# A fused attention and gated feed-forward block on one core: first query tile by key halves, first LayerNorm on VectorE alone, feed-forward weights shared by tiles 0 and 1

## The chip, the core and the metric

The kernel runs on one core of a Trainium2 chip. A core has five engines, each with its own queue of instructions that it works through in order: TensorE (PE: matmul, with weight loads, PEld, that overlap), VectorE (DVE), ScalarE (ACT), GpSimd (POOL) and SyncE (SP), which here issues nearly all DMAs. They meet only at semaphores. Matmul results land in PSUM, from where VectorE or ScalarE copies them to SBUF, the working memory of 128 partitions. The metric is the device time of one execution in microseconds (us), lower is better.

## The reference

The input x has 2048 tokens of width 1024, in bf16. There are 32 query heads of width 32 and a single key/value head that all of them share.

```
def _A_ref(x, wq, wk, wv, wo):
    q = (x @ wq).reshape(B, S, H, Dh) -> (B, H, S, Dh)
    k = x @ wk                       # one head for all
    v = x @ wv
    p = softmax(q k^T * Dh ** -0.5)  # over all 2048 keys, no mask
    return heads_joined(p @ v) @ wo
def _B_ref(x, w_gate, w_up, w_down):
    h = sigmoid(x @ w_gate) * (x @ w_up)     # width 3584
    return h @ w_down
h  = x + _A_ref(layernorm(x), ...)
h2 = h + _B_ref(layernorm(h), ...)
```

## The kernel before

**Order of work.** The program builds its instruction lists with a planner (class Plan, line 37): every operation is given an estimated duration, its dependencies and a priority, a simulated clock decides which operation an engine takes next, and what comes out is a fixed list for each engine, with semaphore waits put in from the dependencies. The loop from line 878 on chooses for TensorE: a score visit if ScalarE has less than 750 ns of work ahead, with a PV block after it if one is ready; otherwise matmuls of the first group that is ready in the order of PRIO (line 376): transposes, K/V, the first Q groups, output projection, gate/up, down, other Q groups. If nothing is ready it plans a filler matmul (line 944; before the first visit that of line 939), which is why fillers show where TensorE had no work.

**Units.** Tokens are cut into 16 tiles of 128. A tile's heads are cut into four pairs of head groups, so there are 64 values of G; G // 4 is the query tile. A visit (G, kq) computes the scores of that pair against 256 keys (emit_S, line 547): 8 small matmuls into PSUM, then two exponentials on ScalarE (line 571), each 128 x 1024, into slots of Pr. Before the change the visits go through G in order and through all eight key blocks kq within it (line 523), and slot u % 16 is used by exponential u. Thus the first pair needs all keys within its eight visits.

**Softmax sums and PV.** VectorE adds the eight key blocks of exponentials into Ts (flush_sums, line 588: seven additions for each of two halves). mk_PV (line 609) makes two blocks of 32 matmuls per G, one for each half of the keys; the second also holds 8 matmuls of a matrix of ones with Ts, which give the row sums. The copies at lines 633 to 645 join the halves, invert the sums and write OT. P slots are reused once their PV block and their addition are done (s_ready, line 531).

**Around attention.** The first LayerNorm is the loop of lines 355 to 367: statistics and centring on VectorE, two pow operations on GpSimd (339, 341), the scale on ScalarE or VectorE as SCALE_ON says. Tiles 0 to 5 (NPT) are transposed on TensorE with a ScalarE copy (line 391), the others by DMA transposes issued from SyncE (line 404). mk_Q (457) computes Q for a head group; all but the first 256 tokens' Q goes through a scratch tensor in DRAM (477) and comes back a tile at a time (516). mk_OP (698) is the output projection and second LayerNorm, flush_hT (725) its transposed copy hnT, mk_GU (788) one item of gate or up, mk_D (840) the down projection.

**Weights.** Each gate or up item for a panel p of 512 columns needs four pieces of 256 KB (USES). A ring of 22 slots keeps pieces; refill (752) replaces the one whose next use is furthest, and ITEMS runs the seven panels upwards for even tiles and downwards for odd ones. The ring shares its memory with x. Weight loads are put into one first-in-first-out line (pace, 244) that pump (248) empties at a planned rate: 260 bytes per ns, and PACE = 205 once more than 64 visits are done. Into the same line go wo (496) and the 28 pieces of w_down (486), the last of these when all Q groups are done (free_wd, 505); gate/up of tile 0 waits for that too (line 835).

Of the kernel before, what the change touches and what calls it, by code (L numbers as in the profile page):

```python
# [9 lines left out]
F32 = mybir.dt.float32  # L10
# [3 lines left out]
P = 128  # L14
# [114 lines left out]
def bass_sequential_preLN__grouped_kv_mqa__glu_gated_glu__prompt_kernel(  # L129
# [22 lines left out]
    ITEMS = [(p, w) for t in range(NT) for p in (range(NFP) if t % 2 == 0 else reversed(range(NFP))) for w in range(2)]  # L152
# [5 lines left out]
    NPS = 16  # L158
    NB = 3
# [4 lines left out]
    USES = [(p, w, d) for p, w in ITEMS for d in range(NPI)]  # L164
# [4 lines left out]
    with ExitStack() as es:  # L169
# [59 lines left out]
        NQS = NFT * 256 // 512  # L229
        half = cst[:, 0:1]  # L230
        negone = cst[:, 1:2]
# [16 lines left out]
        def pump(t):  # L248
            while paced and t >= next_piece[0] and pl.dma_free["sp"] < t + 2500.0:
# [5 lines left out]
                next_piece[0] = max(next_piece[0] + nbytes / (PACE if 64 < v < NV else 260.0), t - 1000.0)  # L255
# [14 lines left out]
        c1 = pl.op("pool", lambda: POOL.memset(negone, -1.0), [c0], occ=60)  # L270
        c2 = pl.op("pool", lambda: POOL.memset(ident[:, :], 0.0), [c1], occ=200)
# [7 lines left out]
        wq_ld = []  # L279

        def load_x(ts):
            sl = slice(ts[0] * P, (ts[-1] + 1) * P)
            o = dma(lambda: SP.dma_start(x_sb[:, ts[0]:ts[-1] + 1, :], xf[sl, :].rearrange("(a p) n -> p a n", p=P)),
                    f"x{ts[0]}", P * D * 2 * len(ts), prio=0)
            for t in ts:
                x_ld[t] = o

        def load_wq(k):
            wq_ld.append(dma(lambda: SP.dma_start(
                wq_sb[:, :, k * 512:(k + 1) * 512],  # L290
                A_wq[:, k * 512:(k + 1) * 512].rearrange("(a p) n -> p a n", p=P)), f"wq{k}", D * 512 * 2, prio=0))
# [6 lines left out]
                    ring="act")  # L298
        load_x([2, 3])
        load_x([4, 5])  # L300
        load_x([6, 7])
        load_wq(0)
        load_x([8, 9])
        load_x([10, 11])
        load_x([12, 13, 14, 15])
        load_wq(1)
# [9 lines left out]
        def stats(ph, ts, srcs, deps, prio):  # L316
            cs = []
            for t, src, dep in zip(ts, srcs, deps):
# [19 lines left out]
            nb = negone if n == 1 else negone.to_broadcast([P, n])  # L338
            g = pl.op("pool", lambda: POOL.tensor_tensor(
                out=dsb[:, ph, sl], in0=zb[:, ph, sl], in1=hb, op=ALU.pow), [f, c0], prio=prio - 1, occ=720, lat=840)  # L340
            h = pl.op("pool", lambda: POOL.tensor_tensor(  # L341
                out=rstd[:, ph, sl], in0=dsb[:, ph, sl], in1=nb, op=ALU.pow), [g, c1], prio=prio - 1, occ=540, lat=660)
            return e, h
# [10 lines left out]
        SCALE_ON = ["dve"] + ["act"] * 7 + ["dve", "act"] * 2 + ["dve"] * 4  # L354
        for ts in [[0], [1]] + [[t, t + 1] for t in range(2, NT, 2)]:
            sv = stats(0, ts, [x_sb[:, t, :] for t in ts], [[x_ld[t]] for t in ts], 3)
            for t in ts:
# [43 lines left out]
        NPT = 6  # L401
# [8 lines left out]
        def queue_after_xT(t):  # L410
# [5 lines left out]
            if t == 3:  # L416
                for g in range(NG):
                    queues["Q"].append(mk_Q(g, 256, 256))
            if t % 4 == 3 and t > 3:
                for g in range(NG):  # L420
                    queues["Q"].append(mk_Q(g, (t // 4) * 512, 512))
# [3 lines left out]
        q_left = [4 * NG + NG]  # L425
        q_left4 = [2 * NG, NG, NG, NG]
# [30 lines left out]
        def mk_Q(g, tok, n):  # L457
# [4 lines left out]
            def after(b, last):  # L462
# [8 lines left out]
                else:  # L471
# [4 lines left out]
                    ev = evac(fa, fd, n, deps, 4)  # L476
# [6 lines left out]
            first = lambda: [wq_ld[g // 4]] + [xT_ev[k] for k in range(tok // P, (tok + n) // P)]  # L483
# [7 lines left out]

        def early_loads(last):
            n = 5 * NG - q_left[0]
            if n in (10, 12):
                k = (n - 10) // 2
                for g in range(4 * k, 4 * k + 4):
                    pace(lambda g=g: SP.dma_start(wo_sb[:, g, :], A_wo[g * P:(g + 1) * P, :]), f"wo{k}", P * D * 2,
                         [last, xT_ev[NT - 1]], wo_ld)
# [24 lines left out]
        visits = [(G, kq) for G in range(NT * ND) for kq in range(VPG)]  # L523
# [3 lines left out]
        slot_add = {}  # L527
        pv_done = {}
        n_exp_of = collections.Counter()

        def s_ready(v):
# [6 lines left out]
            for i in range(2):  # L538
                own = slot_owner.get((2 * v + i) % NPS)
                if own is not None and (own not in pv_done or slot_add.get((2 * v + i) % NPS) is None):  # L540
                    return None
# [3 lines left out]
            return deps  # L545

        def emit_S(v):
# [14 lines left out]
            for i in range(2):  # L562
                u = 2 * v + i
                slot = u % NPS
                own = slot_owner.get(slot)
                free = [pv_done[own], slot_add[slot]] if own is not None else []
# [5 lines left out]
                    out=Pr[:, slot, :].rearrange("p (a b) -> p a b", a=2), in_=S_ps[:, pb:pb + 2, :],  # L572
# [13 lines left out]
        sum_todo = collections.deque((G, kq) for G in range(NT * ND) for kq in range(1, VPG))  # L586

        def flush_sums():
            while sum_todo:
                G, kq = sum_todo[0]  # L590
                if n_exp_of[G] <= kq or (kq == 1 and G > 1 and (G - 2, 1) not in pv_done):
                    return
                sum_todo.popleft()
                for i in range(2):
                    T = Ts[:, G % 2, i * 1024:(i + 1) * 1024]
                    ins = [kq - 1, kq] if kq == 1 else [kq]
                    src = [Pr[:, slot_of[(G, q, i)], :] for q in ins]
                    deps = [exp_of[(G, q, i)] for q in ins]
                    deps.append(pv_done.get((G - 2, 1)) if kq == 1 else sum_ev[(G, kq - 1, i)])
# [5 lines left out]
                    sum_ev[(G, kq, i)] = o  # L605

        oc_ev = {}

        def mk_PV(G, h):
            qb, g = G // ND, 2 * (G % ND)  # L610

            def block(b):
                r = []
                for kt in range(8 * h, 8 * h + 8):
                    kq, kk = kt // KB, kt % KB
                    for j in range(4):
                        slot = slot_of[(G, kq, j // 2)]
                        co = (j % 2) * 512 + kk * 256
                        r.append(mm(F_ps[DH * j:DH * (j + 1), b, 0:256], Vb[:, kt, :], Pr[:, slot, co:co + 256],
# [434 lines left out]
```

## Time and profile before

Three executions took 1127.34 to 1129.27 us, median 1128.49. The profiled one took 1126.47 us, of which the span from first to last instruction is 1124.7 us; the granted TensorE clock averaged 0.998.

| Engine | busy us | share of span | instructions |
|---|---|---|---|
| TensorE matmul | 1069.6 | 95% | 12163 |
| TensorE weight load | 478.9 | 43% | 12347 |
| VectorE | 873.7 | 78% | 1690 |
| ScalarE | 1022.9 | 91% | 1165 |
| GpSimd | 49.1 | 4% | 84 |

| Group (line) | count | busy us | mean ns |
|---|---|---|---|
| exponentials, ScalarE (571) | 1024 | 961.9 | 1056 |
| later row-sum additions, VectorE (601) | 768 | 509.0 | 677 |
| first row-sum additions, VectorE (601) | 128 | 85.4 | 681 |
| gate/up matmuls with ring weights (379) | 1659 | 414.3 | 381 |
| down matmuls (379) | 839 | 208.9 | 380 |
| tanh, ScalarE (817) | 112 | 71.1 | 635 |
| LN1 scale on ScalarE (363) | 9 | 10.0 | 1141 |
| LN1 scale on VectorE (366) | 7 | 3.2 | 480 |
| reciprocal of row sums, VectorE (640) | 64 | 12.3 | 192 |

Busy time counts overlapping instructions once, so a mean can exceed the spacing: a matmul of 381 ns in the table is followed by the next after some 0.22 us. Some matmul records are missing from the trace. A busy TensorE is not one at its peak, and fillers count as busy. In forty equal slices of the span, the busy tenths of ScalarE and the share of the DMA engines are:

```
ACT  6799989999999999999999999999999999999210
DMA  7776188887959597786959596796959596875992
```

ScalarE is full from the fifth slice until near the end; the last exponential starts at 1045.0 us. The first starts at 30.9 us, the first projection with wo at 108.1, the first gate/up matmul at 139.9.

### The profile page before, as it was taken

How to read it: one execution, taken by the hardware profiler on the slowest of the kernel's cores; microseconds unless marked ns; L12 is line 12 of the kernel's file. 1: busy time of each engine (PE TensorE's matmuls, PEld its weight loads, DVE VectorE, ACT ScalarE, POOL GpSimd, SP SyncE). 2: the span in 40 equal slices, each digit the busy share in tenths (PEclk: the TensorE clock that was granted, in tenths of full speed). 3: DMA queues.
4: the chain of work that ended last, by engine and by line, in shares of the span. 5: the costliest groups of instructions: out<-in, count | busy, mean ns of one | idle time of the engine just before them, and what ended most of it. 6: DMA issues, size and time to landing. Idle time of an engine off the chain costs nothing.

```text
span 1124.7 us, 30157 instructions
## 1 busy us (share of the span) xinstructions
PE 1069.6 (95%) x12163; PEld 478.9 (43%) x12347; DVE 873.7 (78%) x1690; ACT 1022.9 (91%) x1165; POOL 49.1 (4%) x84
## 2 busy tenths in 40 slices
PE   9899889999999999999999999999999999999998
PEld 5643344444444444444444444444444444444443
DVE  8889878787887878787887878887888878788411
ACT  6799989999999999999999999999999999999210
POOL 4100000000000000000000000000000000000000
PEclk9999999999999999999999999999999999999999
DMA  7776188887959597786959596796959596875992
GB/s 241 156 250 194 59 255 228 214 237 188 253 131 262 146 245 202 190 229 155 246 138 256 129 262 184 206 229 162 239 143 253 126 259 171 222 204 160 248 276 63
DMA packets 302651, 225.22 MB, mean 200 GB/s; under 512 B 117424, under 2 KB 293808, under 8 KB 302512
## 3 DMA queue, kind: packets, MB, share of 16 engines
q1 hardware_dynamic: 300432, 223.15, 75.7%
q8 instruction: 97, 1.59, 0.6%
q10 hardware_dynamic: 2080, 0.13, 0.1%
q14 instruction: 42, 0.34, 0.1%
HBM read 193.86 MB, written 7.86 MB: 179 GB/s over the span
## 4 chain that ended last, share of the span: by engine, by line
PE 82%; ACT 5%; DVE 5%; issue 5%; DMA 2%; POOL 0%; SPq 0%; DVEq 0%; ACTq 0%
PE F_ps L379 69%; PE S_ps L379 14%; ACT Pr L571 5%; DVE Ts L601 2%; DMA ring<-in_B_w_gate_dram 1%; DMA ring<-in_B_w_up_dram 1%; DVE st L320 1%; DVE st L322 1%; ACT ring L363 0%; DVE ring L359 0%; DMA ring<-in_A_x_dram 0%; DVE hact L267 0%; ACT tnh L817 0%; DVE Rc L639 0%; POOL rstd L341 0%
## 5 line engine op out<-in xcount | busy, mean ns | idle before, releaser
L571 ACT ACTIVATE Pr<-S_ps 128x1024 bf16<-128x1024 f32 x1024 | 961.9, 1056 | 18.2 <-PE S_ps L379 15.3
L601 DVE TENSOR_TENSOR Ts<-Ts,Pr 128x1024 bf16<-128x1024 bf16 x768 | 509.0, 677 | 46.7 <-ACT Pr L571 42.2
L379 PE MATMUL F_ps<-ring,hnT 128*128 128x512 bf16 x1659 | 414.3, 381 | 18.8 <-issue 12.2
L379 PEld LDWEIGHTS F_ps<-ring,hnT 128*128 128x128 bf16 x1754 | 150.4, 98 | 219.7 <-issue 74.3
L379 PE MATMUL S_ps<-QTb,kT 32*128 32x256 bf16 x4096 | 203.5, 273 | 14.5 <-ACT Pr L571 7.0
L379 PE MATMUL F_ps<-zone,hact 128*128 128x512 bf16 x839 | 208.9, 380 | 4.5 <-issue 4.3
L821 DVE SCALAR_TENSOR_TENSOR hst<-tnh,F_ps 128x512 bf16<-128x512 f32 x112 | 76.4, 682 | 93.0 <-PE F_ps L379 86.2
L379 PEld LDWEIGHTS S_ps<-QTb,kT 32*128 32x128 bf16 x4096 | 60.7, 92 | 193.4 <-ACT Pr L571 133.2
L379 PE MATMUL F_ps<-Pr,Vb 128*32 128x256 bf16 x4096 | 135.9, 275 | 2.9 <-DVE hact L267 1.1
L601 DVE TENSOR_TENSOR Ts<-Pr 128x1024 bf16<-128x1024 bf16 x128 | 85.4, 681 | 51.9 <-ACT Pr L571 51.7
L379 PEld LDWEIGHTS F_ps<-zone,hact 128*128 128x128 bf16 x896 | 77.0, 97 | 105.5 <-issue 33.2
L817 ACT ACTIVATE tnh<-F_ps 128x512 f32<-128x512 f32 x112 | 71.1, 635 | 50.4 <-PE F_ps L379 50.4
L379 PEld LDWEIGHTS F_ps<-Pr,Vb 128*32 128x32 bf16 x4096 | 97.9, 97 | 40.7 <-DVE hst L821 11.8
L379 PE MATMUL F_ps<-zone 128*128 128x256 bf16 (+2 forms) x500 | 72.8, 287 | 5.7 <-DVE Rc L639 2.0
L379 PE MATMUL F_ps<-wo_sb,OT 128*128 128x512 bf16 x240 | 59.8, 380 | 3.1 <-issue 2.1
L334 POOL TENSOR_SCALAR zb<-mvb 128x1 bf16<-128x1 bf16 (+1 forms) x25 | 10.8, 430 | 1012.6 <-DVE mvb L330 1012.6
L379 PEld LDWEIGHTS F_ps<-zone 128*128 128x128 bf16 x512 | 37.4, 97 | 33.2 <-issue 9.1
L851 DVE SCALAR_TENSOR_TENSOR h_sb<-F_ps,h_sb 128x512 bf16<-128x512 f32 x32 | 22.0, 688 | 34.3 <-PE F_ps L379 28.7
L379 PEld LDWEIGHTS F_ps<-wo_sb,OT 128*128 128x128 bf16 x256 | 22.4, 98 | 29.9 <-issue 6.5
L637 DVE TENSOR_TENSOR Oc<-F_ps,Oc 128x256 f32<-128x256 f32 x64 | 26.8, 419 | 4.2 <-PE F_ps L379 4.1
L639 DVE STREAM_TRANSPOSE Rc<-F_ps 128x256 f32<-128x256 f32 x64 | 28.1, 439 | 0.0
L642 DVE STREAM_TRANSPOSE Rc<-Ri 128x256 f32<-128x256 f32 x64 | 27.9, 436 | 0.0
(48 smaller groups left out, 348.8 us busy)
## 6 DMA issues: line engine op xcount, KB each, us to landing
ring<-in_B_w_gate_dram SPq DMA_DIRECT2D x316, 256.0 KB, 3.8
ring<-in_B_w_up_dram SPq DMA_DIRECT2D x315, 256.0 KB, 3.9
zone<-in_B_w_down_dram SPq DMA_DIRECT2D x28, 256.0 KB, 4.0
h_sb<-in_A_x_dram SPq DMA_DIRECT2D x16, 256.0 KB, 5.0
out_dram<-h_sb SPq DMA_DIRECT2D x32, 128.0 KB, 3.0
QTb<-q_scratch SPq DMA_DIRECT2D x14, 256.0 KB, 4.4
q_scratch<-hact SPq DMA_DIRECT2D x24, 128.0 KB, 2.6
ring<-in_A_x_dram SPq DMA_DIRECT2D x5, 512.0 KB, 7.1
```

The costliest lines, as they stand in the source:

```text
L320: a = pl.op("dve", lambda k=k, src=src: DVE.bn_stats(st[:, k, 0, :], src[:, 0:512]), dep, prio=prio, occ=590, lat=756, order=[st_user.get(k)])
L322: b = pl.op("dve", lambda k=k, src=src: DVE.bn_stats(st[:, k, 1, :], src[:, 512:1024]), dep, prio=prio, occ=590, lat=756, order=[st_user.g ...
L334: f = pl.op("pool", lambda: POOL.tensor_scalar(out=zb[:, ph, sl].unsqueeze(2), in0=mvb[:, ph, sl, 1:2], scalar1=LN_EPS_BF16, scalar2=None, ...
L379: return lambda: PE.matmul(o, lhsT=l, rhs=r, start=start, stop=stop, **kw)
L571: exps[u] = pl.op("act", lambda slot=slot, pb=pb: ACT.activation(out=Pr[:, slot, :].rearrange("p (a b) -> p a b", a=2), in_=S_ps[:, pb:pb ...
L601: o = pl.op("dve", lambda T=T, a=a, b=b: DVE.tensor_tensor(out=T, in0=a, in1=b, op=ALU.add), deps, prio=4, **t_dve(1024, 1.92))
L637: a = pl.op("dve", lambda: DVE.tensor_tensor(out=Oc[:, :], in0=O, in1=Oc[:, :], op=ALU.add), [last, oc_ev[G]], prio=0, **t_dve(256))
L639: c = pl.op("dve", lambda: DVE.transpose(out=Rc[:, :], in_=R), [last, o_ev.get(G - 1)], prio=0, **t_dve(256))
L642: d = pl.op("dve", lambda: DVE.transpose(out=Rc[:, :], in_=Ri[:, :].unsqueeze(2).to_broadcast([P, 2 * P // DH, DH])), [r], prio=2, **t_dve ...
L817: tanh_of[n] = pl.op("act", lambda: ACT.activation(out=tnh[:, n % 2, :], in_=F_ps[:, b, :], func=ACTF.Tanh, scale=0.5), [last, tn_user.get ...
L821: e = pl.op("dve", lambda: DVE.scalar_tensor_tensor(out=hst[:, n % NST, :], in0=tnh[:, n % 2, :], scalar=1.0, in1=F_ps[:, b, :], op0=ALU.a ...
L851: e = pl.op("dve", lambda: DVE.scalar_tensor_tensor(out=h_sb[:, t % 4, sl], in0=F_ps[:, b, :], scalar=0.5, in1=h_sb[:, t % 4, sl], op0=ALU ...
```

## The change

Seven edits that come together:

1. Four pairs of head groups (NX = 4, the first query tile) are visited key half by key half: first half of pairs 0 and 1 in turn, then of 2 and 3, then all second halves. Their row sums no longer come from VectorE additions: each PV block also multiplies its exponentials by ones. First-half results wait in OcX, which lies in the memory of wo, as do four more P slots; slots are now taken from a free list. wo is therefore loaded only after pair 3.
2. For the other sixty pairs the two halves of Ts are merged by one more VectorE addition, and 4 instead of 8 ones-matmuls follow.
3. LN1 scales all run on VectorE, and the second pow on GpSimd becomes a reciprocal on VectorE, for both LayerNorms.
4. Two tiles instead of six are transposed on TensorE; the first two tiles' statistics are taken as a pair.
5. x and wq are loaded in other portions, the later ones only once the statistics of an earlier pair are done.
6. Q for tokens 512 to 1023 is computed in groups of 256 tokens, and Q copies have priority 1 instead of 4.
7. Tiles 0 and 1 run their gate/up panels interleaved, and the pace of weight loads is 280, or 205 only after visit 120.

```diff
-    ITEMS = [(p, w) for t in range(NT) for p in (range(NFP) if t % 2 == 0 else reversed(range(NFP))) for w in range(2)]
+    TP = [(0, p) for p in range(5)] + [(1, 4), (1, 3), (0, 5), (1, 5), (0, 6), (1, 6)] + [(1, p) for p in (2, 1, 0)]
+    TP += [(t, p) for t in range(2, NT) for p in (reversed(range(NFP)) if t % 2 else range(NFP))]
+    ITEMS = [(t, p, w) for t, p in TP for w in range(2)]
...
+        OcX = wo_sb[:, 0:4, :].rearrange("p a b -> p (a b)").bitcast(F32).rearrange("p (a b) -> p a b", a=NX)
+        def pslot(sl):
+            return Pr[:, sl, :] if sl < NPS else wo_sb[:, 4 + sl - NPS, :]
...
-                next_piece[0] = max(next_piece[0] + nbytes / (PACE if 64 < v < NV else 260.0), t - 1000.0)
+                next_piece[0] = max(next_piece[0] + nbytes / (PACE if 120 < v < NV else 280.0), t - 1000.0)
...
+        load_wq(0, 2)
         load_x([2, 3])
+        load_wq(2, 4)
         load_x([4, 5])
-        load_x([6, 7])
-        load_wq(0)
-        load_x([8, 9])
-        load_x([10, 11])
-        load_x([12, 13, 14, 15])
-        load_wq(1)
...
-            h = pl.op("pool", lambda: POOL.tensor_tensor(
-                out=rstd[:, ph, sl], in0=dsb[:, ph, sl], in1=nb, op=ALU.pow), [g, c1], prio=prio - 1, occ=540, lat=660)
-            return e, h
+            h = pl.op("dve", lambda: DVE.reciprocal(rstd[:, ph, sl], dsb[:, ph, sl]), [g], prio=prio - 1, occ=90, lat=250)
+            return e, h, cs[-1]
...
-        SCALE_ON = ["dve"] + ["act"] * 7 + ["dve", "act"] * 2 + ["dve"] * 4
-        for ts in [[0], [1]] + [[t, t + 1] for t in range(2, NT, 2)]:
+        SCALE_ON = ["dve"] * 16
+        for ts in [[t, t + 1] for t in range(0, NT, 2)]:
             sv = stats(0, ts, [x_sb[:, t, :] for t in ts], [[x_ld[t]] for t in ts], 3)
+            if ts[0] + 6 < NT:
+                load_x([ts[0] + 6, ts[0] + 7], [sv[2]])
+            if ts[0] == 0:
+                load_wq(4, 8, [sv[2]])
...
-        NPT = 6
+        NPT = 2
...
-            if t == 3:
+            if 1 < t < 8 and t % 2 == 1:
                 for g in range(NG):
-                    queues["Q"].append(mk_Q(g, 256, 256))
-            if t % 4 == 3 and t > 3:
+                    queues["Q"].append(mk_Q(g, (t - 1) * P, 256))
+            if t % 4 == 3 and t > 8:
...
-                    ev = evac(fa, fd, n, deps, 4)
+                    ev = evac(fa, fd, n, deps, 1)
...
-        visits = [(G, kq) for G in range(NT * ND) for kq in range(VPG)]
+        visits = [(G + i, kq) for G in range(0, NX, 2) for kq in range(VPH) for i in range(2)]
+        visits += [(G, kq) for G in range(NX) for kq in range(VPH, VPG)]
+        visits += [(G, kq) for G in range(NX, NT * ND) for kq in range(VPG)]
...
-        sum_todo = collections.deque((G, kq) for G in range(NT * ND) for kq in range(1, VPG))
+        sum_todo = collections.deque((G, kq) for G in range(NX, NT * ND) for kq in range(1, VPG))
...
+                if kq == VPG - 1:
+                    T4 = Ts[:, G % 2, :].rearrange("p (a k b) -> p a k b", a=4, k=KB)
+                    merge_ev[G] = pl.op("dve", lambda T4=T4: DVE.tensor_tensor(
+                        out=T4[:, :, 0, :], in0=T4[:, :, 0, :], in1=T4[:, :, 1, :], op=ALU.add),
+                        [sum_ev[(G, kq, i)] for i in range(2)], prio=3, **t_dve(1024, 1.92))
...
+                        if G < NX:
+                            rs.append(mm(F_ps[DH * j:DH * (j + 1), b, 256:512], ones[:, :], pslot(slot)[:, co:co + 256],
+                                         kt == k0, kt == k1 - 1, tile_position=(0, DH * j)))
+                for j in range(4 if G >= NX and h else 0):
+                    r.append(mm(F_ps[DH * j:DH * (j + 1), b, 256:512], ones[:, :],
+                                Ts[:, G % 2, j * 512:j * 512 + 256], True, True, tile_position=(0, DH * j)))
...
+                    if G == NX - 1:
+                        load_wo([last] + x_users)
...
-            gr.gate = lambda: ready() is not None and (q_left[0] == 0 if t == 0 else (t < 2 or d_done[t - 2] == 2))
+            gr.gate = lambda: t in hT_ev and ready() is not None and (q_left[0] == 0 if t < 2 else d_done[t - 2] == 2)
```

## The prediction

> **What bounds the kernel now.** I read four views in this order: the busy time by stage, the chain of waits, the groups of instructions in two windows, and SyncE's timeline where TensorE ran dry. First the stages (columns: window; its length; busy us and instructions of TensorE, weight loads, VectorE, ScalarE, GpSimd; granted clock; DMA share; GB/s):
>
> ```profile
> 31.00:50.00 19.00, 16.24 (x260) 12.31 (x258) 18.64 (x49) 14.09 (x16) 3.87 (x6) 1.00 0.66 152
> 50.00:140.00 90.00, 82.43 (x1028) 37.20 (x1039) 79.99 (x154) 86.80 (x95) 2.02 (x3) 1.00 0.55 168
> 140.00:220.00 80.00, 71.87 (x881) 32.94 (x896) 61.23 (x116) 75.50 (x87) 1.92 (x3) 0.98 0.84 233
> 312.70:375.50 62.80, 60.66 (x725) 26.38 (x733) 51.12 (x98) 62.59 (x73) 2.08 (x3) 1.00 0.81 200
> 1045.00:1124.70 79.70, 75.19 (x388) 33.89 (x385) 18.15 (x33) 7.13 (x12) 1.35 (x3) 1.00 0.74 194
> ```
>
> 312.7:375.5 is one query tile of the steady part. ScalarE is full (62.59 of 62.8): 64 exponentials plus 7 tanh, so an exponential costs (62.8 - 7 x 0.635) / 64 = 0.91 us. But the exponentials end at 1046, and 79 us of feed-forward matmuls follow them. The chain of waits, as shares of the span by engine:
>
> ```profile
> PE 82%; ACT 5%; DVE 5%; issue 5%; DMA 2%; POOL 0%; SPq 0%; DVEq 0%; ACTq 0%
> ```
>
> and two of the tail's pieces from the same chain in order of time (start, us, what, how many):
>
> ```profile
> 1072.32 10.74 PE F_ps L379 x49
> 1083.11 10.79 PE F_ps L379 x49
> ```
>
> The tail runs at 10.74 / 49 = 0.219 us for a 512-column matmul. The last tile alone needs 16 + 112 + 56 = 184 of them, 40 us; the other 39 us are a backlog. So the end is set by **TensorE work not yet done when the exponentials stop**. A us of TensorE time won anywhere before is a us off the end, while ScalarE may shift by up to some 39 us without being felt.
>
> Where TensorE loses time is seen by comparing 140:220 (first three rows) with the steady tile (last three):
>
> ```profile
> L379 PE MATMUL F_ps<-ring,hnT 128*128 128x512 bf16 x145 | 38.1, 382 | 5.8 <-DMA ring<-in_B_w_up_dram 3.5 <-issue 1.7 <-DVE Oc L633 0.3
> L379 PE MATMUL F_ps<-kT,ident 128*128 128x256 bf16 x57 | 8.5, 286 | 0.6 <-DVE Rc L639 0.6
> L379 PE MATMUL F_ps<-wo_sb,OT 128*128 128x512 bf16 x15 | 3.7, 380 | 0.2 <-DVE Ts L601 0.2
> ...
> L379 PE MATMUL F_ps<-ring,hnT 128*128 128x512 bf16 x106 | 26.5, 380 | 0.8 <-issue 0.8
> L379 PE MATMUL F_ps<-zone,hact 128*128 128x512 bf16 x52 | 13.3, 381 | 0.3 <-issue 0.3
> L379 PE MATMUL F_ps<-wo_sb,OT 128*128 128x512 bf16 x15 | 3.7, 380 | 0.2 <-issue 0.2
> ```
>
> The steady tile passes 173 recorded wide matmuls in 62.8 us, thus 220 in 80 us; 140:220 has 160. Sixty are missing, 60 x 0.219 = **13 us**, and 57 filler matmuls (all between 156 and 201) stand where they should be. SyncE's timeline names the cause:
>
> ```profile
> 142.87 5.24 SPq L488 DMA_DIRECT2D zone<-in_B_w_down_dram  x6
> 148.85 1.20 SPq L825 DMA_TRANSPOSE hact<-hst  x1
> 150.11 3.07 SPq L488 DMA_DIRECT2D zone<-in_B_w_down_dram  x5
> 154.18 1.20 SPq L825 DMA_TRANSPOSE hact<-hst  x1
> 155.60 0.40 SPq L488 DMA_DIRECT2D zone<-in_B_w_down_dram  x1
> 156.04 0.94 SPq L775 DMA_DIRECT2D ring<-in_B_w_up_dram  x2
> ```
>
> The last Q group ends at 139.9; 16 down-projection pieces go first; no gate or up piece is fetched until 156, when the 22 resident ones are used up. From there line 255 paces at 205 bytes/ns, 256 KB every 1.28 us.
>
> The other loss is the start: by 50 us only 16 exponentials are done (1 before 31, 15 in 31:50), and TensorE has finished 6 transposed tiles, 8 K/V groups, 8 first Q groups, one more Q group, 8 visits and one PV block.
>
> **The change, part by part.** Sums are in TensorE time, against the profiled run's own 1126.5 us (span 1124.7 and 1.8 around it).
>
> Start. LN1 now wholly on VectorE adds 9 scales at 0.48 us and 8 reciprocals at 0.19 to it, 5.8 us, and takes 9 x 1.14 us and four PSUM copies at 1.02, 14.4 us, from ScalarE; GpSimd loses the second pow. Per pair VectorE needs 4 x 0.64 of statistics, 0.4 of aggregates, 0.3 of casts, 4 x 0.43 of centring and scaling and 0.19: 5.2 us, so pair p is normalised near 9 + 5.2p. Tiles 0 and 1 pass TensorE and ScalarE by about 12, K/V and Q group 0 follow, first exponential near 16 instead of 30.9. Tiles 2 to 15 go by DMA transpose on SyncE: 14 issues instead of 10 at 1.3 us, landing after 3.3; one pair takes 2.6 of each 5.2 us, so SyncE keeps up. X loads held back by a pair's aggregates start some 15 us before VectorE wants them; behind them on SyncE stand only the wq pieces for groups 4 to 7, needed near 20 us and sent near 7. The last keys are there near 9 + 36 + 3 + evacuations, 50 to 55 us, no sooner than before (kT at 49.4). What changes is that 32 exponentials (29 us) need only pairs 0 to 3 instead of 8: ScalarE is fed from 16 to 50. By 50 us it has done 28 to 32 instead of 16, about **13 us ahead**. TensorE has Q for tokens 256 to 1023 from 19 us on. Wall work done by 50 us before: K/V 8 x 1.4, Q 9 x 0.87, 8 visits x 0.33, one PV 0.9: 22.5 us, apart from 3.7 of transposes. Available now is 36 us from 14 on; at 0.85 (the steady tile fills 184 x 0.219 + 32 x 0.33 + 8 x 0.88 + 4 x 0.22 = 58.8 of 62.8, 0.94; I go lower because VectorE is full) that is 30.6. **-8 us**; bounds 0 (evacuations stay stuck behind LN) and -12.
>
> A rule speaks against this part: the Trainium skill, Perfetto Trace Analysis, "Optimizing Scalar/DVE Operations", says that when VectorE is saturated some of its work may be given to ScalarE; the change does the reverse, while VectorE is busy 18.64 of 19 us. By the rule the start loses 5.8 us of VectorE time to keys that come later: -2. By the trace ScalarE is the one that holds things: in 10:31 K, Q and transposed copies stand in its queue between LN scales of 1.14 us, and VectorE sheds the 7.9 us of row sums it did before 50. I follow the trace.
>
> Row sums. In the first four pairs 64 ones-matmuls replace 8: 4 x 56 x 27.5 ns (PV takes 0.88 us for 32) = **+6.2 us**. VectorE is rid of 56 additions at 0.68, 38 us, before 80 us. TensorE waited for VectorE there (31:140, hact 3.1, Rc 2.0, Oc 1.1 and smaller, 7 us); Q copies also rise to priority 1. Half of it: **-3.5**; bounds 0 and -7. Sixty later pairs issue 4 ones-matmuls instead of 8: 240 x 27.5 ns = **-6.6**. Their merge is no row of this trace; nearest is L601, the same 1024 bf16 elements, 0.68 us: 41 us on VectorE, raising it from 51.1 to 53.8 of 62.8. Behind a merge on VectorE stand the next additions and PSUM copies that free TensorE's banks. TensorE's own and its weight loads' waits on VectorE are about 33 us for 874 busy, 4%; so **+1.6**, bounds 0 and +41. The second-half PV waits some 0.9 us more; its slots are first needed four visits (7.8 us) later.
>
> Weights. Tile 0 runs panels 0 to 4, tile 1 takes 4 and 3 from the ring, and so on: 18 new pieces at first instead of 34, and the pace is 280 (0.94 us a piece). Q ends near 140 as before: 8 + 3.5 won, 6.2 spent on sums, 4 on visits that come earlier. Then 16 down pieces take 15 us while 22 resident ones last 22 x 0.438 / 0.64 = 15 (0.64 is the wide share of the steady tile). The 18 need 16.9 us against 12.3 for TensorE: 4.6 x 0.64 = 2.9 us lost. The same sum for before gives 34 x 1.28 = 43.5 against 28.8 (output projection included), 9.4, where 13 was measured; scaled, 4 stay. **-9**; bounds -4 and -13. The new wait is panel 4 of tile 1 on tile 1's transposed h: due near 140 + 37, ready near 172 (tile 1's attention ends 13 us sooner; 17 us from output projection to hnT as in tile 0). Only covered by 5 us; behind it the whole GU queue would stand, us for us. Wo, loaded only after pair 3 (near 81), lands near 93, hnT near 113; Q until 140 hides 27 us of lateness.
>
> The clock rule: TensorE: Matmul & The Clock Gate, "Why this matters for your kernels", says that idle gaps over about 3 us drop the clock. The stage row has 0.98 for 140:220, within which one tile window reads 0.91: a dip worth about 1.7 us at most. If the new order left a gap the rule would add as much; with fewer DMA waits I take it as gone, inside the 9.
>
> Sum: -8 + 6.2 - 3.5 - 6.6 + 1.6 - 9 = -19.3; 1107.2 profiled. The median shown stands 2.0 above the profiled run, so **1109**.
>
> **Rivals.** (A) The merges land on TensorE: each delays a bank's release by its whole 0.68 us. Then +39.4, 1148; slower than before from about half of it (0.33 us a merge). For: VectorE at 86%, one queue. Against: the 4%. (B) VectorE holds the start: Q and K copies queue behind LN, no gain there: 1117. For: 18.64 of 19. (C) DMA, not the pace, limits 140:220 (share 0.84, and 0.91 at 270 GB/s in 140:160), or the tile-1 wait bites: 9 us stay, 1118. (D) Both losses vanish: -4 and -4 more, the VectorE waits too: 1098. That the sharing does nothing is part of C: 649 pieces (631 into the ring, 18 into P slots) should fall by about 15.
>
> **Chances.** Mine 0.52 (own range 1101 to 1117), B 0.17, C 0.12, D 0.09, A 0.10. About 0.2% (2.3 us) is what a measurement can tell. Of B and C 0.03 end within it and 0.02 above, where both meet. Faster 0.85, same 0.03, slower 0.12. The range 1096 to 1126 leaves out A and the edges.
>
> **What would show it.** First exponential near 16; 28 to 32 done by 50; last exponential near 1033; few fillers in 140:220 and over 200 wide matmuls there; tail still over 70 us. Wrong, if waits of TensorE on VectorE grow beyond 40 us, if a gap stands ahead of tile 1's panel 4, or if the tail grows by what the start gains.

## The result, and the profile after

The changed kernel took 1109.59 to 1111.14 us in four executions, median 1110.95, beside 1127.91 (1126.82 to 1129.27) for the kernel before: a ratio of 0.9846, interval 0.9829 to 0.9863, thus 17.4 us less. The forecast was 1109. The profiled execution took 1111.14 us (span 1109.1), 15.3 less than the profiled one before, where the sum of the prediction had 19.3.

The busy time by stage of the changed kernel, with the columns that the same view of before had (window; length; busy us and instructions of TensorE, weight loads, VectorE, ScalarE, GpSimd; granted clock; DMA share; GB/s):

```profile
31.00:50.00 19.00, 16.68 (x280) 11.96 (x278) 16.58 (x50) 17.32 (x24) 3.18 (x7) 1.00 0.99 179
50.00:140.00 90.00, 86.73 (x1322) 46.72 (x1333) 63.81 (x132) 88.25 (x97) 1.52 (x2) 1.00 0.62 186
140.00:220.00 80.00, 74.51 (x905) 33.30 (x912) 66.94 (x126) 79.02 (x93) 1.33 (x2) 1.00 1.05 269
312.70:375.50 62.80, 60.79 (x715) 26.14 (x720) 53.64 (x103) 62.64 (x72) 1.14 (x2) 1.00 0.80 200
1033.00:1109.10 76.10, 70.73 (x320) 31.53 (x325) 14.86 (x26) 5.37 (x9) 0.79 (x2) 1.00 0.75 189
```

ScalarE is busy 17.32 of the 19 us ahead of 50 us (14.09 before), VectorE falls from 79.99 to 63.81 in 50:140, and 140:220 moves 269 GB/s instead of 233. The steady tile is all but unchanged; its TensorE column must not be read as idle time, for matmul records are missing from both traces. hidden_merge, a kernel further down with the same TensorE list and all records, is busy 62.80 of 62.8 us there. The chain of waits, as shares of the span, is still TensorE's:

```profile
PE 82%; ACT 8%; issue 4%; DVE 4%; DMA 2%; SPq 0%; POOL 0%; POOLq 0%
```

Its end, in order of time (start, us, what, how many matmuls):

```profile
1030.35 4.84 DMA ring<-in_B_w_gate_dram
1035.24 9.89 PE F_ps L384 x45
...
1066.77 7.73 PE F_ps L384 x35
1074.52 5.10 DMA ring<-in_B_w_gate_dram
1079.66 9.89 PE F_ps L384 x45
```

The last exponential starts at 1027.3 instead of 1045.0, and 81.8 us of feed-forward follow it (79.7 before), still at 9.89 / 45 = 0.22 us a matmul, but twice the chain passes through a transfer of a gate piece (once before the change, at 1047.0).

To see where the time came from I count, in both traces, the weight loads of wide (512-column) matmuls, whose records are complete, and the exponentials, started by a given time:

| by (us) | wide before | wide after | exponentials before | exponentials after |
|---|---|---|---|---|
| 50 | 0 | 0 | 15 | 24 |
| 140 | 18 | 29 | 109 | 119 |
| 220 | 191 | 238 | 185 | 198 |
| 375.5 | 646 | 685 | 342 | 357 |
| 1020 | 2528 | 2582 | 998 | 1016 |

By 140 us TensorE is 11 wide matmuls ahead (11 x 0.219 = 2.4 us), 10 exponentials with their visits and PV (2.8 us, at an estimated 0.275 each from 0.33 a visit and 0.88 a PV block), and has done the 6.2 us of sums from P besides. By 220 it is 47 wide (10.3 us) and 13 exponentials (3.6) ahead, by 1020 it is 54 wide (11.8) and 18 exponentials (5.0): 16.8 us, of which the span shows 15.6. So 13.9 of the 16.8 us were there by 220, and the 800 us that follow, in which fewer ones-matmuls should have told, added 2.9.

The groups of TensorE in 140:220, after the change (line, operation, tiles, count | busy us, mean ns | idle before and what ended it):

```profile
L384 PE MATMUL F_ps<-ring,hnT 128*128 128x512 bf16 x178 | 44.7, 381 | 4.1 <-issue 2.4 <-DMA ring<-in_B_w_up_dram 1.1 <-DVE Rc L680 0.4
...
L384 PE MATMUL F_ps<-kT,ident 128*128 128x256 bf16 x27 | 3.6, 274 | 0.3 <-DVE Oc L663 0.3
```

178 recorded gate/up matmuls stand where 145 stood, 27 fillers instead of 57, and the wait for up pieces falls from 3.5 to 1.1 us. SyncE's timeline shows what is left of the cause:

```profile
144.29 2.94 SPq L493 DMA_DIRECT2D zone<-in_B_w_down_dram  x6
...
151.17 0.82 SPq L493 DMA_DIRECT2D zone<-in_B_w_down_dram  x2
152.04 2.74 SPq L817 DMA_DIRECT2D ring<-in_B_w_up_dram  x2
...
171.81 1.32 SPq L769 DMA_TRANSPOSE hnT<-hn  x1
```

The first up piece leaves at 152 instead of 156, still behind the down pieces, and tile 1's transposed h (hnT) leaves at 171.8, to land 4.1 us later, at 176.0. TensorE's timeline at both places (start, us, what, count):

```profile
151.75 2.03 PE L384 MATMUL F_ps<-kT,ident 128*128 128x256 bf16 x17
...
174.30 1.25 PE L384 MATMUL F_ps<-ring,hnT 128*128 128x512 bf16 x5
175.39 0.49 PE L384 MATMUL F_ps<-kT,ident 128*128 128x256 bf16 x3
...
177.13 0.50 PE L384 MATMUL F_ps<-kT,ident 128*128 128x256 bf16 x3
```

21 fillers around 151 are the pieces that haven't come; six around 176 are tile 1's hnT, for which nothing was left in hand. Both walls of this stage are thus visible in one row of matmuls.

### The profile page after: what moved, and what is told of

The parts are those of the page before. It is cut to its first block, busy times and chain, and to the rows that moved or that the text cites. A ratio compares the mean times of both kernels' runs of the same rounds, so it can differ in the third digit from the quotient of the medians.

```text
span 1109.1 us, 29973 instructions
## 1 busy us (share of the span) xinstructions
PE 1061.8 (96%) x12140; PEld 475.8 (43%) x12306; DVE 884.5 (80%) x1727; ACT 1011.6 (91%) x1162; POOL 27.9 (3%) x56
## 4 chain that ended last, share of the span: by engine, by line
PE 82%; ACT 8%; issue 4%; DVE 4%; DMA 2%; SPq 0%; POOL 0%; POOLq 0%
PE F_ps L384 68%; PE S_ps L384 14%; ACT Pr L588 8%; DMA ring<-in_B_w_gate_dram 1%; ACT tnh L860 1%; DVE Ts L618 1%; DMA ring<-in_B_w_up_dram 1%; DVE st L325 1%; DVE st L323 0%; DVE ring L371 0%; DVE ring L364 0%; DVE hact L274 0%; SPq L817 0%; DVE hst L864 0%; DVE mv L327 0%
## 5 line engine op out<-in xcount | busy, mean ns | idle before, releaser
L588 ACT ACTIVATE Pr<-S_ps 128x1024 bf16<-128x1024 f32 x1014 | 951.4, 1054 | 6.6 <-PE S_ps L384 5.6
L618 DVE TENSOR_TENSOR Ts<-Ts,Pr 128x1024 bf16<-128x1024 bf16 x720 | 475.3, 679 | 40.6 <-ACT Pr L588 36.9
L384 PE MATMUL F_ps<-ring,hnT 128*128 128x512 bf16 x1671 | 418.4, 381 | 19.3 <-issue 11.7
L618 DVE TENSOR_TENSOR Ts<-Pr 128x1024 bf16<-128x1024 bf16 x120 | 80.5, 688 | 37.3 <-ACT Pr L588 37.1
L384 PEld LDWEIGHTS F_ps<-zone 128*128 128x128 bf16 x576 | 42.6, 97 | 29.5 <-issue 8.8
L625 DVE TENSOR_TENSOR Ts<-Ts 128x1024 bf16<-128x1024 bf16 x60 | 41.4, 689 | 1.5
```

The source lines that it names most:

```text
L384: return lambda: PE.matmul(o, lhsT=l, rhs=r, start=start, stop=stop, **kw)
L588: exps[u] = pl.op("act", lambda slot=slot, pb=pb: ACT.activation(out=pslot(slot).rearrange("p (a b) -> p a b", a=2), in_=S_ps[:, pb:pb + 2 ...
L618: o = pl.op("dve", lambda T=T, a=a, b=b: DVE.tensor_tensor(out=T, in0=a, in1=b, op=ALU.add), deps, prio=4, **t_dve(1024, 1.92))
L625: merge_ev[G] = pl.op("dve", lambda T4=T4: DVE.tensor_tensor(out=T4[:, :, 0, :], in0=T4[:, :, 0, :], in1=T4[:, :, 1, :], op=ALU.add), [sum ...
```

## The experiments

Theory: three separate amounts, TensorE time won at the start by the key halves, TensorE time won in 140:220 by the shared panels and the faster pace, and fewer ones-matmuls, with the merges hidden. Rivals: the merges cost TensorE time; the tile-1 wait eats what the sharing brings; scaling LN on VectorE holds the start. All edits are made to the changed kernel. The differences below are those of the ratios times 1128 us, against the changed kernel's 0.9846; with two intervals of about 0.0015 each, they are uncertain by some 2 us. "Wide by 220" is the count of the table above (238). Edits 4, 5 and 6 and the reciprocal of edit 3 were not taken out one by one.

**Sharing and pace.**

```diff
# share_off
-    TP = [(0, p) for p in range(5)] + [(1, 4), (1, 3), (0, 5), (1, 5), (0, 6), (1, 6)] + [(1, p) for p in (2, 1, 0)]
-    TP += [(t, p) for t in range(2, NT) for p in (reversed(range(NFP)) if t % 2 else range(NFP))]
+    TP = [(t, p) for t in range(NT) for p in (reversed(range(NFP)) if t % 2 else range(NFP))]
# pace_old
-                next_piece[0] = max(next_piece[0] + nbytes / (PACE if 120 < v < NV else 280.0), t - 1000.0)
+                next_piece[0] = max(next_piece[0] + nbytes / (PACE if 64 < v < NV else 260.0), t - 1000.0)
# share_pace_off: both
```

> The changed kernel with tiles 0 and 1 running their gate/up panels one after the other again (up, then down), at the new pace of 280. My theory (TensorE work before the last exponential decides; the supply of weight pieces after the Q groups is what starved it): the pace did most of it, because 34 pieces at 0.94 us are 31.8 us against 28.8 us of TensorE time; 1 to 4 us slower than the changed kernel, 1112 to 1115. Rival (the DMA engines, not the planned pace, were the limit, so fewer pieces is what helped): all 7 us that 140 to 220 us won are lost, 1118 or more, with 50 to 60 fillers.

> The changed kernel with the old pace (260, and 205 after visit 64), panels still shared. My theory: 18 pieces at 1.28 us are 23 us against 12.3 us of TensorE time, some 5 us lost: 1114 to 1118, fillers 45 to 60. Rival (fewer pieces is what helped, the pace is not felt): 1111, fillers near 27.

> The changed kernel with both the old panel order and the old pace. Both theories: the whole loss of before is back, 57 fillers or more, 7 to 10 us slower than the changed kernel: 1118 to 1121. If it is slower still, the earlier attention of tile 1 makes the starved stretch worse; if it stays at 1111, the gain does not come from the weights at all.

Measured: without sharing 0.9880 (+3.8 us), wide by 220 224; with the old pace 0.9832 (-1.6), 235, where my theory had 3 to 7 us more; without both 1.0026 (+20.3), 204. In 140:220 sharing and pace are substitutes: one alone missing costs 14 or 3 wide matmuls (3.1 or 0.7 us), both missing 34, or 7.4 us. That is the stage's worth, near the 9 forecast. But the third kernel lost 20 us, not 7: its ten steady tiles (375.5 to 1003.3 us) passed 1795 wide matmuls instead of 1848, 11.6 us, though the edits touch nothing there but the order in which the planner arrives. This recurs below.

**Key halves.**

```diff
-    NX = 4
+    NX = 0
...
+            if n == 10:
+                load_wo([last, xT_ev[NT - 1]])
```

> The changed kernel without its first part: visits in the order of G and then key block, all row sums by VectorE additions, no extra P slots, wo loaded with the early loads. All other parts stay. My theory: the start's 8 us and the 3.5 us of VectorE relief are lost and the 6.2 us of ones-matmuls come back: about 5 us slower than the changed kernel, 1114 to 1118, with 16 to 18 exponentials by 50 us. Rival (the lead of ScalarE is what counts): all 15 us that its last exponential came earlier are lost, 1124 to 1127.

Measured: 0.9964 (+13.3 us), more than the 5 us of my theory; 12 exponentials by 50 us instead of 24; wide by 220 197 (41 fewer, 9.0 us) and 14 exponentials fewer with their visits and PV (3.9 us), together 12.9; the steady tiles 1845, all but unchanged. The first exponential stays at 19.9. TensorE's timeline of this kernel shows what ScalarE's lost lead costs:

```profile
121.60 1.48 PE L384 MATMUL F_ps<-kT,ident 128*128 128x256 bf16 x12
...
133.29 0.81 PE L384 MATMUL F_ps<-ring,hnT 128*128 128x512 bf16 x3
...
166.54 1.59 PE L384 MATMUL F_ps<-kT,ident 128*128 128x256 bf16 x13
...
175.18 0.38 PE L384 MATMUL F_ps<-wo_sb,OT 128*128 128x512 bf16 x1
```

and SyncE's:

```profile
127.37 1.58 SPq L771 DMA_TRANSPOSE hnT<-hn  x1
```

Without the sums from P, TensorE is through with Q by 114, but tile 0's attention isn't: its hnT leaves at 127.4, and fillers run until 133. From 160 to 175 fillers run again: tile 1's output projection begins only at 175.2, when tile 1's attention is done, and its gate/up stands behind that. 230 fillers ran in all, 32 in the changed kernel. The key halves are worth more than their own TensorE time, since they bring the end of attention of tiles 0 and 1 forward to where the other work runs out.

**Row sums on VectorE.** Three ways to ask what a merge costs:

```diff
# two_merges: a second merge per pair, on the path to PV
+                    merge_ev[G] = pl.op("dve", lambda T4=T4: DVE.tensor_tensor(
+                        out=T4[:, :, 1, :], in0=T4[:, :, 0, :], in1=T4[:, :, 1, :], op=ALU.add),
+                        [merge_ev[G]], prio=3, **t_dve(1024, 1.92))
# no_merge: block of the merge removed, eight ones-matmuls again
-                for j in range(4 if G >= NX and h else 0):
+                for kk in range(KB if G >= NX and h else 0):
+                    for j in range(4):
...
# hidden_merge: as much VectorE time again, inside the same planned operation
+                    merge_ev[G] = pl.op("dve", lambda T4=T4, G=G: (DVE.bn_stats(scr[:, G % 16, :], T4[:, 0:2, 1, :]), DVE.tensor_tensor(
...
```

> The changed kernel with a second, useless VectorE addition of the merge's size behind each of the sixty merges, ahead of the second-half PV block. It doubles the merge's 41 us on VectorE. My theory (VectorE has room, 4% of its time is felt by TensorE): 1 to 3 us slower than the changed kernel, that is 14 to 16 us below before. Rival (merges land on TensorE by late bank releases): 20 to 40 us slower, near or above before.

> The changed kernel with the old form of the row sums for pairs 4 to 63: no merge, 8 ones-matmuls instead of 4. My theory: 240 x 27.5 ns = 6.6 us more on TensorE, 1.6 us less from VectorE: 5 us slower than the changed kernel, 12 us below before. Rival (merges land on TensorE): faster than the changed kernel by up to 30 us.

> The changed kernel's own instruction lists, in the same order on every engine, with one more VectorE instruction of some 0.68 us put directly ahead of each of the sixty merges without the planner knowing. It prices 41 us of VectorE work with no change of plan, which adding a planned instruction could not. My theory (4% of VectorE's time is felt by TensorE): 1 to 3 us slower than the changed kernel. Rival (the merges land on TensorE): 20 to 40 us slower.

Measured: two merges 0.9811 (-3.9 us, faster), no merge 1.0043 (+22.2), the hidden work 0.9849 (+0.3). The first two have opposite signs to any price of a merge, and their counts tell why: up to 220 us they stand at 237 and 230, but in the ten steady tiles they pass 1858 and 1771 wide matmuls against 1848. A merge that the planner sees changes every later choice that it makes, and so the list. The third is the clean one: TensorE's and ScalarE's lists are the same as in the changed kernel, VectorE gets the extra work that the planner does not see, and it costs 0.3 us, nothing that can be told from zero. The row of the merge in the changed kernel (line, operation, shapes, count | busy, mean ns | idle before):

```profile
L625 DVE TENSOR_TENSOR Ts<-Ts 128x1024 bf16<-128x1024 bf16 x60 | 41.4, 689 | 1.5
```

As much VectorE work again as these 41.4 us is hidden, though it stands on the same path to PV. The rival that puts it on TensorE falls. What the first merge costs alone isn't measured, since taking it out changes the list.

**Ones-matmuls.**

```diff
# hidden_ones: each ones-matmul of pairs 4 to 63 issued twice, in the same planned list
-                    r.append(mm(F_ps[DH * j:DH * (j + 1), b, 256:512], ones[:, :],
-                                Ts[:, G % 2, j * 512:j * 512 + 256], True, True, tile_position=(0, DH * j)))
+                    m = mm(F_ps[DH * j:DH * (j + 1), b, 256:512], ones[:, :], Ts[:, G % 2, j * 512:j * 512 + 256], True, True, tile_position=(0, DH * j))
+                    r.append(lambda m=m: (m(), m())[1])
# few_p_sums: one key tile's sums from P instead of all, in the first four pairs
-                        if G < NX:
+                        if G < NX and kt == k0:
...
-                                         kt == k0, kt == k1 - 1, tile_position=(0, DH * j)))
+                                         True, True, tile_position=(0, DH * j)))
```

> The changed kernel's own lists with each of the 240 ones-matmuls of pairs 4 to 63 issued twice, unknown to the planner; order otherwise the same. My theory (TensorE time counts one for one wherever it falls): 240 x 27.5 ns = 6.6 us slower than the changed kernel. Rival (in the steady part TensorE waits for ScalarE anyway): under 2 us slower.

> The changed kernel that leaves out seven eighths of the row sums of the first four pairs (one ones-matmul group for each PV block instead of eight; the first tile's softmax is then scaled wrongly). 448 - 64 = 224 matmuls less in pairs whose old form had 32: what is saved against the changed kernel is 4 x 56 x 27.5 ns = 6.2 us of TensorE time before 100 us. My theory (TensorE time anywhere before the last exponential counts one for one): 6 us faster, 23 us below before, and some 28 more wide matmuls done by 220 us. Rival (ScalarE's order sets the start and TensorE has slack there): under 2 us.

Measured: 240 ones-matmuls more cost 4.5 us by the ratio (0.9886) and 5.8 in the profiled spans (1114.9 against 1109.1), thus 19 to 24 ns each, where 27.5 were assumed. So TensorE time is felt at about 0.7 to 0.9 of its length (with 2 us of uncertainty on 6.6), with no change of list. Without most of the sums from P the time was 0.9842 (-0.5), not 6 us less. Gate/up began at 129.8 instead of 136.0, ran into the missing pieces sooner (fillers from 143 to 154) and into tile 1's hnT (fillers from 169 to 173): 66 fillers instead of 32, and 14 more wide by 220, half of the 6.2 us freed. The other half is lost in the steady tiles (1832 instead of 1848), with another list again. TensorE time won ahead of a wall is worth only what the wall leaves.

**Down pieces out of the way.** The last 16 pieces of w_down are held until item 9 of gate/up:

```diff
-                    load_wd(4 * i, 4, [last])
+                    if i < 3:
+                        load_wd(4 * i, 4, [last])
+                    else:
+                        wd_hold.append((4 * i, last))
...
+                if i == 9:
+                    for f, dep in wd_hold:
+                        load_wd(f, 4, [dep])
```

> The changed kernel in which the last 16 down-projection pieces enter the line of loads only after panel 4 of tile 0, so that gate/up pieces go first once Q is done. My theory (those 16 pieces are what still starves TensorE at 150 to 180 us): the 27 fillers of 140 to 220 go below 8, 10 to 20 more wide matmuls by 180 us, 2 to 4 us faster, 19 to 21 us below before. Rival (the DMA engines' rate or tile 1's transposed h is the limit): fillers stay above 20, no difference beyond 1 us.

Measured: 1.0038 (+21.7 us), where 2 to 4 us less were expected. SyncE's timeline of this kernel, and then TensorE's:

```profile
164.82 11.52 SPq L493 DMA_DIRECT2D zone<-in_B_w_down_dram  x13
176.64 1.26 SPq L773 DMA_TRANSPOSE hnT<-hn  x1
```

```profile
161.79 1.04 PE L384 MATMUL F_ps<-ring,hnT 128*128 128x512 bf16 x4
...
172.77 1.59 PE L384 MATMUL F_ps<-kT,ident 128*128 128x256 bf16 x13
...
180.08 1.59 PE L384 MATMUL F_ps<-kT,ident 128*128 128x256 bf16 x13
...
182.39 1.24 PE L384 MATMUL F_ps<-ring,hnT 128*128 128x512 bf16 x5
```

From 140 to 162 no filler runs: the down pieces were what starved the stage. Then the line of gate/up items stands at tile 1's first panel from 168.5 to 182.4, until its hnT, issued at 176.6, has landed. That hnT is itself 4.8 us later than in the changed kernel, and not for the 13 down pieces issued just ahead of it: VectorE finished hn only at 176.6. 222 wide are done by 220 instead of 238: with the first wall gone, TensorE only comes to the second one sooner. The remaining 18 us were lost later (1773 wide in the steady tiles).

**LN scales back on ScalarE.**

```diff
-        SCALE_ON = ["dve"] * 16
+        SCALE_ON = ["dve"] + ["act"] * 7 + ["dve", "act"] * 2 + ["dve"] * 4
```

> The changed kernel with nine of the first LayerNorm's sixteen scales back on ScalarE (1.14 us each) and off VectorE (0.48 each). To be read at the start, since the plan of the rest moves too. My theory: ScalarE again delays K, Q and the first exponentials: first exponential after 22 us, 18 to 21 exponentials by 50 instead of 24, 10 to 20 wide matmuls fewer by 220 us. Rival (VectorE is the one that is full, so spreading helps): keys earlier, 25 or more exponentials by 50, as many wide matmuls by 220.

Measured: 1.0054 (+23.5 us), first exponential at 21.8 instead of 19.8, 22 by 50 us instead of 24, wide by 220 220 (18 fewer, 3.9 us); steady tiles 1781. The early part went as expected, and scaling on VectorE is right here, although VectorE was the fuller engine at the start before the change (18.64 of 19 us, ScalarE 14.09). Most of the 23.5 is again a steady part that the edit does not touch.

**The tail's pace.**

```diff
-                next_piece[0] = max(next_piece[0] + nbytes / (PACE if 120 < v < NV else 280.0), t - 1000.0)
+                next_piece[0] = max(next_piece[0] + nbytes / (PACE if 120 < v < NV else (280.0 if v < NV else 260.0)), t - 1000.0)
```

> The changed kernel with the pace of 280 kept until the last visit and the old 260 after it. TensorE's, VectorE's and ScalarE's lists are the same as the changed kernel's; only SyncE's order of some late loads differs. My theory (two waits of TensorE for gate pieces near 1030 and 1075 us are what the pace costs in the tail, since old pace throughout was 4.7 us shorter in span): 2 to 5 us faster than the changed kernel. Rival (the gap between the two is luck of the plan elsewhere): within 1 us of it.

Measured: 0.9841 (-0.6 us), inconclusive. TensorE's waits for gate pieces after 1027 fell from 3.0 to 0.6 us and the profiled span by 3.5, but the medians don't show it.

**Why four kernels lost 20 us in a part they don't touch.** share_pace_off, no_merge, wd_late and ln_scale_act all end 1.8 to 2.1% above the changed kernel, with 53 to 77 fewer wide matmuls between 375.5 and 1003.3 us. I read the order of TensorE's work there from the traces: between two visits, how many wide matmuls stand and whether a PV block does; then, at what share of visits this is the same 32 visits later, one query tile on.

| kernel | same one tile later | wide, ten tiles | ratio |
|---|---|---|---|
| before | 0.99 | 1839 | 1 |
| after | 0.99 | 1848 | 0.9846 |
| two_merges | 1.00 | 1858 | 0.9811 |
| pace_old | 0.96 | 1852 | 0.9832 |
| key_order_old | 0.98 | 1845 | 0.9964 |
| few_p_sums | 0.86 | 1832 | 0.9842 |
| share_off | 0.32 | 1836 | 0.9880 |
| share_pace_off | 0.23 | 1795 | 1.0026 |
| no_merge | 0.23 | 1771 | 1.0043 |
| wd_late | 0.19 | 1773 | 1.0038 |
| ln_scale_act | 0.17 | 1781 | 1.0054 |

One list that doesn't repeat and one that does, side by side: waits in 375:1003 of the kernel without merges (engine, line, what was waited for: us in total, times, longest):

```profile
PEld F_ps L384 <- DMA ring<-in_B_w_up_dram: 7.0, 6, 1.5
ACT Pr L588 <- PE S_ps L384: 6.8, 14, 1.2
...
PE F_ps L384 <- DMA ring<-in_B_w_up_dram: 4.9, 6, 1.3
PEld F_ps L384 <- DVE Rc L677: 4.9, 6, 1.1
```

and of the changed kernel, which has no row for the pieces in that stretch:

```profile
PEld F_ps L384 <- DVE Rc L685: 1.9, 9, 0.2
ACT Pr L588 <- PE S_ps L384: 0.4, 1, 0.4
```

All six lists that repeat at 0.86 or more lie below all four slow ones in time, and of the lists that don't repeat only share_off was spared the loss. This goes together in eleven kernels; it is not shown as the cause, since no kernel was run in which the order alone was forced to repeat, and what makes the planner fall out of step wasn't tried.

two_merges was faster than the changed kernel (1104.12 us, its interval 0.9798 to 0.9824 apart from the changed kernel's); pace_old (1107.41), few_p_sums and tail_260 stand lower too, with overlapping intervals. The extra merge is dead work: its gain lies in the list that the planner happens to make with it, 6 wide matmuls ahead of the changed kernel's at 375.5 us and 16 (3.5 us) at 1020. The stretch of ten tiles of two_merges, of hidden_merge (with the changed kernel's list) and of no_merge (columns as in the first view):

```profile
375.50:1003.30 627.80, 627.80 (x7200) 261.30 (x7199) 572.32 (x1072) 627.80 (x719) 15.14 (x20) 1.00 0.76 200
...
375.50:1003.30 627.80, 626.16 (x7167) 259.05 (x7160) 561.68 (x1064) 626.74 (x714) 11.59 (x20) 1.00 0.80 200
...
375.50:1003.30 627.80, 612.71 (x7179) 255.59 (x7175) 513.21 (x975) 620.50 (x706) 12.72 (x20) 1.00 0.74 190
```

In these three traces every matmul is recorded. Both good lists leave TensorE idle for less than 2 us; no_merge leaves 15.1 (wd_late 15.9, ln_scale_act 15.2). The changed kernel's own trace has 608.03 us in this stretch, but only 7048 matmuls for 7142 weight loads: that gap is one of records, not of work.

## Why the prediction was right, and where its steps were not

The time and the likeliest case were right: -17.4 us by the ratio, -15.3 profiled, against -19.3. By stage, the counts give 5.2 us by 140 us (the first three terms sum to 5.3), 8.7 in 140:220 (9), 2.9 from there to 1020 (5.0), and 1.2 lost again in the tail (nothing forecast). That the first pair meets so closely is partly luck, since the times beneath it were off. Step by step:

- **Bound.** "A us of TensorE time won anywhere before is a us off the end" held at 0.7 to 0.9 in the steady part (hidden_ones), and at the start only as far as the walls in 140:220 let it (few_p_sums: -0.5 us for 6.2 freed). "ScalarE may shift by up to some 39 us without being felt" failed in the early part: a ScalarE that is 12 exponentials later at 50 us and 14 at 220 makes tiles 0 and 1 end later, and TensorE has nothing else then (key_order_old, 230 fillers). For the steady part no run tests it.
- **Start, -8, and relief of VectorE, -3.5.** Together 11.5; counted by 140 us 2.4 + 2.8, and with the 6.2 of sums from P as computed 11.4. The picture beneath was too bright: the first exponential came at 19.8, not 16, and 24 were done by 50, not 28 to 32. TensorE's waits for VectorE in 31:140 fell from 7.2 to 3.1 us, 4.1 where 3.5 was taken. Nor is all of it the key halves': without them and with all else kept (key_order_old), 44 wide and 102 exponentials are started by 140, against 18 and 109 before, a lead of 5.7 - 1.9 = 3.8 us. ScalarE's lead at the end was 17.7 us, not 13.
- **Sums from P, +6.2.** Not measured by itself: it is taken as computed in the 11.4. The step treats it as a loss at the end, us for us, and few_p_sums shows half of it being eaten by the walls behind.
- **The two steps as a block.** The sum gives the key halves -8 + 6.2 - 3.5 = -5.3; taking them out cost 13.3. The edits cover for one another: without the halves, the shared panels stand at tile 1's hnT as well.
- **Fewer ones-matmuls, -6.6, and merges, +1.6.** The merge took 0.69 us, as taken, and as much VectorE work again cost 0.3 us, where 1.6 was taken for the first; 240 ones-matmuls are worth 4.5 (both to some 2 us). This is the mis-sized term of the sum: 5.0 forecast, and 16.8 - 13.9 = 2.9 us found between 220 and 1020 in the accounting above. In ten steady tiles the changed list passed 9 wide matmuls more than before, 2.0 us. It does not show where the rest went: TensorE has no idle time that could hold it (hidden_merge, 626.16 of 627.80 us), and 2 us is near what these counts can tell.
- **Weights, -9.** From 140 to 220 the wide count rose from 173 to 209: 36 x 0.219 = 7.9 us, with 3 exponentials more 8.7; with both edits undone 34 are missing by 220 (7.4 us). The reading that sixty were missing was made on incomplete matmul records, but holds on complete weight loads (173 against 234 in 80 us of the steady tile). Over 200 wide in the stage held; "few fillers" came out as 27. Pieces fell by 16 from 649 to 633 (15 forecast). wo's loads were issued from 93.3 (93 for their landing), hnT of tile 0 at 118.9 (113). The row's clock of 0.98 became 1.00: the dip went, and no gap brought it back. It stood behind a wait shorter than the rule's (last section).
- **The tile-1 wait, "only covered by 5 us".** The cover was used up: due at 175.4, landed at 176.0, six fillers. It was rightly named as what comes next, and wd_late ran into it for 14 us.
- **The rule that speaks against the change** (the Trainium skill, Perfetto Trace Analysis, "Optimizing Scalar/DVE Operations": work of a saturated VectorE may go to ScalarE). With the scales back on ScalarE 18 fewer wide matmuls were done by 220: the trace's answer was the better one here. No time for the whole kernel can be drawn from it.
- **Rivals.** A is refuted by hidden_merge, and the sign set for it did not come: waits of TensorE and its weight loads on VectorE fell from 36 to 27 us, instead of growing beyond 40. B's sign is there (the first exponential 4 us late) without its loss. C's wait exists but left the stage 7.4 to 8.7 of the 9 us. D's last 4 and 4 did not come: both walls still show fillers.
- **Tail.** Still over 70 us, and it grew by 2.1 us, with two waits for gate pieces on the chain instead of one; whether the pace of 280 makes them stays open.

## What to carry to other kernels

Where a planner writes fixed lists, an edit's total can be six times what its own place is worth (ln_scale_act: 23.5 us for 3.9): compare work done by the end of the edited stage, ask whether the steady part's order repeats, and price an operation by putting a second one into the list behind the planner's back. Before reading idle time from a trace, compare its matmuls with its weight loads: some hundred missing records looked like 20 us of idle TensorE here. A stage that starves has more than one wall: before removing a wait, work out when the next dependency is ready, because TensorE time won ahead of it only brings the engine there sooner. An engine with slack at the end of the kernel can still be the one that sets the start.

## What the runs showed of the hardware that was not expected

- VectorE took 41 us more work (60 pieces of 0.69 us, on an engine busy 85% of the steady tile) for 0.3 us of time, with an uncertainty of some 2 us.
- The DMA engines moved 269 GB/s over 80 us in 140:220 beside everything else, 233 before, and TensorE's waits for pieces fell.
- 128x32 ones-matmuls of 256 columns cost 19 to 24 ns each when added (to some 8 ns), though one alone is recorded at 272 ns: they overlap about twelvefold in the record.
- Before the change the granted clock was 0.83 in 160:170, behind TensorE's longest wait of the stage, 2.5 us for an up piece until 160.8; in the changed kernel the longest there is 1.1 us, and the clock 1.00. That is shorter than the "about 3 us" of the clock rule in the prediction, and wd_late dips to 0.83 in 810:820 behind a gap of 2.0 us. But key_order_old had a gap of 2.5 us at 42.8 and kept 1.00 in 40:50: the traces show no threshold.
- Kernels with the changed kernel's TensorE list (hidden_merge, tail_260) differ from it by up to 5 wide matmuls at the times of the table, about 1 us: smaller differences of this count are not read.
